# Loading the output gradient earlier, with rotating tables and four store buffers, in a spectral block's forward and backward kernel

## The chip, the cores and the metric

The kernel runs on one core of one Trainium2 chip. The metric is the time of one execution on the device in microseconds, lower is better. A core has TensorE (PE, with its weight loads shown as PEld), VectorE (DVE), ScalarE (ACT), GpSimd (POOL) and SyncE (SP), each working through its own list of instructions in order, and 16 DMA engines. Nearly all transfers of this kernel are issued from SP's queue.

## The reference

The reference computes one transformer-like block in bf16 and the gradients of all its weights and of its input. The sequence has 2048 rows of 512.

```
h = layernorm(x) * (1 + ca) + sa
x = x + ga * irfft2(rfft2(h) * (w_r + i w_i))        # spectral filter
h = layernorm(x) * (1 + cb) + sb
x = x + gb * (relu(h @ w1 + b1)**2 @ w2 + b2)        # MLP, 512 -> 1792 -> 512
sa, ca, ga, sb, cb, gb = split(silu(c) @ w_mod)      # modulation, six rows of 512
out, vjp = jax.vjp(block, x, w_r, w_i, w1, b1, w2, b2, c, w_mod)
return out, *vjp(grad_out)
```

The outputs that matter here: out_2 and out_3 are the gradients of w_r and w_i, out_4 that of w1, out_5 of b1, out_6 of w2, out_7 of b2, out_1 of x, out_9 of w_mod.

## The kernel before

Rows are laid on 128 partitions, 16 row tiles (NT) of 512 columns. The Fourier transforms are products with small tables. The kernel has these stages, in order of time.

1. To about 100 us: the first layer norm, the forward transforms and the product with the filter (`spec_f23`, `spec_g1`), filled with products of the transposed output gradient with w2 (L707).
2. To about 283 us: for each of four blocks of 512 rows, the inverse transform, the second layer norm, both products of the MLP and the backward of the MLP. The hidden layer and its gradient are stored to `h_dram` and `gh_dram`; the gradient's transposed blocks are loaded back (`ghn`, tiles named gab). The row gradients are kept in `gx1_dram`.
3. To about 337 us, the middle stage on the way back: `spec_f23` is called with `ew_b` and `after_b`. It has eight steps `gi`. In each, PE makes psB and psC (L323, L311), ACT copies them to AE and G (L329, L330, L313), and DVE multiplies G with the filter Z and with the saved spectrum Xt (`cmul`, L418 to L421). The products are stored as the gradients of w_r and w_i from tile gW (L1146). Around that PE works through units of the gradient of w1 (`grad_w1`, L1104), whose result ACT copies into gw1 tiles (L1108) of two units each; they are stored at L1110. Four of the six modulation gradients (`GMod.emit`) are made here, after steps 1, 3, 5 and 7. Each multiplies a broadcast row with w_mod's columns (tile wmc, DVE, L470) and writes an outer product (tile gwm, ACT and DVE, L467 and L469), with two loads and two stores.
4. To the end: `spec_g1` (L346), then eight steps of two row tiles (`row_pair`) with the last transforms (L375, L385), the layer norm's backward on DVE and ACT with the saved rows n1 and gxl (L1193, L1194), and a store of out_1. Around them stand the units of w2's gradient (`grad_w2`, L1173): each reads the whole output gradient `g_sb` (2 MB) and one transposed block of the hidden layer (`hn`, loaded with a transposing DMA at L1168), and DVE takes its PSUM result away (L1176). PSUM pool `mmps` has two buffers. The last two modulation gradients and the gradient of c end the kernel.

On-chip memory is nearly full, so pools are stacked from the left and from the right and re-used. A new pool on old space waits for everything in the pools that lay there. The pools that matter: `gap` (ghn), `gwa` (G, gw1, and the modulation tiles), `spb` (Z), `f23b` (Xb, four buffers), `ewb` (products and gW), `cdp` (Cd, AE and LF tables 0 to 3), `lf2` (LF tables 4 to 7, 6 KB a partition), `gwp` (g_sb with 16 KB a partition, hn, gw) and `fin` (n1, gxl). Pool `gwp` is opened after `lf2` is released, and lies in part where `ewb` was.

The order of instructions on each engine is drawn up at build by a planner: it goes by the order of the program, by priorities (`high_priority`, `Priority`), by when data and buffers come free in its own estimate of time, and by `issue_after`, which queues an instruction behind another on the same engine. On the chip each engine and SP's queue keep that order and wait in place.

Each LF table is read by the psC products of one step (L311). Tables 4 to 7 are loaded in `load(gi)`, which `after_b` calls four steps ahead; the first loads of Z and Xb come from the same function.

Of the kernel before, what the change touches and what calls it, by code (L numbers as in the profile page):

```python
# [12 lines left out]
BF16 = mybir.dt.bfloat16  # L13
# [5 lines left out]
D = 512  # L19
DF = 257  # L20
# [3 lines left out]
NT = 16  # L24
# [3 lines left out]
P = 128  # L28
# [24 lines left out]
class Priority:  # L53


    def __init__(self, tc, shift):
        self.tc, self.shift = tc, shift
# [335 lines left out]
def merge(main, *fills):  # L393

    fill = [f for fl in fills for f in fl]
    k = 0
    for i, m in enumerate(main):
        m()
        while k < len(fill) and k * len(main) < (i + 1) * len(fill):
            fill[k]()  # L400
            k += 1
# [42 lines left out]
class GMod:  # L444
# [2 lines left out]

    def __init__(self, tc, K, scf, gsc, wm_view, out9_view):
        self.__dict__.update(locals())
        self.bufs = 2  # L450

    def emit(self, jc, q, row, pool, ppool):

# [22 lines left out]
def kernel(  # L476
# [5 lines left out]
    nc = tc.nc  # L482
# [14 lines left out]
    g_view = grad_out.rearrange("b (p t) d -> p (b t) d", t=NT)  # L497
# [20 lines left out]
    K = build_basic(tc, constp)  # L518
    mmps = ctx.enter_context(tc.tile_pool(name="mmps", bufs=2, space=PSUM, side="right"))
# [242 lines left out]
    with tc.tile_pool(name="psR", bufs=1, space=PSUM) as psR, tc.tile_pool(name="psO", bufs=2, space=PSUM) as psO_pool, \  # L762
# [92 lines left out]
        def ghn_part(b, fc):  # L855

            if fc == 0:
                tl = gap.tile([P, NFC, SB], BF16, name="gab", bufs=4)
                ghn[b] = tl.rearrange("p a b -> p (a b)").rearrange("p (j f) -> p j f", f=F)
            nc.sync.dma_start(ghn[b][:, :, fc * P:(fc + 2) * P], gh_dram[fc * P:(fc + 2) * P, b * SB:(b + 1) * SB], transpose=True)  # L860
# [149 lines left out]
        for b in range(NB):  # L1010
            again0, again = f1_again(UT) if b == NB - 1 else ([], [])
            if b < NB - 1:
                m = stage_m(0) if b == 0 else []
                stage_h(b, m + stage_g(b + 1), 2 if b == 0 else 6)
            else:
                late.lag = 2
                stage_h(b, again0, 2)
            parts = [lambda fc=fc: ghn_part(b - 1, fc) for fc in range(0, NFC, 2)] if b > 0 else []
            if b < NB - 1:
                merge(stage_o(b), stage_m(b + 1) + [lambda: None] * 2)  # L1020
                if b == NB - 2:
                    UT = utcs.tile([P, 4, 16, NT, 8], BF16, name="utcs")
                merge(stage_gn(b, UT), parts + [lambda: None])
            else:
                w1p.release()
                cdp = tc.alloc_tile_pool(name="cdp", bufs=1, side="right")
                K["Cd"] = cdp.tile([P, D], BF16, name="Cdb")
                nc.sync.dma_start(K["Cd"], Cd_dram)
                AEs = make_ae(nc, cdp)
                K["LF"] = [cdp.tile([P, 2, 3, P], BF16, name=f"LFb{gi}") for gi in range(4)]  # L1030
                for gi in range(4):
                    nc.sync.dma_start(K["LF"][gi], LF_dram[:, 2 * gi:2 * gi + 2])
                merge(stage_gn(b, UT), [x for p in zip(again, parts + [lambda: None]) for x in p])
                w1tp.release()
                h2p = tc.alloc_tile_pool(name="h2p", bufs=1, side="right")
                h2_sb = h2p.tile([P, NT, D], BF16, name="h2_sb")
                nc.sync.dma_start(h2_sb, h2_dram)
                parts = [lambda fc=fc: ghn_part(b, fc) for fc in range(0, NFC, 2)]
                merge(stage_o(b), [x for p in zip([lambda: None] * 3 + [late_f1.flush] + [lambda: None] * 3, parts) for x in p])
# [7 lines left out]


    gm = GMod(tc, K, scf, gsc, wm_view, out9_view)
    lf2 = tc.alloc_tile_pool(name="lf2", bufs=1, side="right")  # L1050
    K["LF"] += [lf2.tile([P, 2, 3, P], BF16, name=f"LFb{gi}") for gi in range(4, 8)]
    W4 = 448
    NFB = F // W4
    gwa = tc.alloc_tile_pool(name="gwa", bufs=1)
# [43 lines left out]
    w1o = {}  # L1098

    def grad_w1(fb, dc):  # L1100
        fs = slice(fb * W4, (fb + 1) * W4)
        ps = mmps.tile([P, SB], FP32, name="mm")
        for t in range(NT):
            nc.tensor.matmul(ps[:, 0:W4], lhsT=h2_sb[:, t, dc * P:(dc + 1) * P], rhs=ghn[t // 4][:, t % 4, fs],  # L1104
                             start=(t == 0), stop=(t == NT - 1))
        if fb % 2 == 0:
            w1o[0] = gwa.tile([P, 2, W4], BF16, name="gw1", bufs=2)
        nc.scalar.copy(out=w1o[0][:, fb % 2, :], in_=ps[:, 0:W4])  # L1108
        if fb % 2 == 1:
            nc.sync.dma_start(out4_view[:, dc, (fb - 1) * W4:(fb + 1) * W4], w1o[0].rearrange("p a f -> p (a f)"))  # L1110
# [8 lines left out]
    def fill_w1(n):  # L1119
        for _ in range(n):  # L1120
            if units:
                units.pop(0)()

    gms = [lambda j=j, q=q, row=row: gm.emit(j, q, row, gwa, mmps)
           for j, q, row in ((5, 0, grow[0:1, :]), (2, 32, grow[32:33, :]), (3, 64, grow[64:65, :]), (4, 0, gcrow))]

    with tc.tile_pool(name="f23b", bufs=2) as fr, tc.tile_pool(name="ewb", bufs=2) as ew:
        Xt = {}

        def load(gi):  # L1130
            if gi >= 4:
                nc.sync.dma_start(K["LF"][gi], LF_dram[:, 2 * gi:2 * gi + 2])
            nc.sync.dma_start(Z[gi], wz_dram[:, gi])
            Xt[gi] = fr.tile([P, 2, 2, FP], BF16, name="Xb", bufs=4)
            nc.sync.dma_start(Xt[gi], xs_dram[:, gi])

        for gi in range(4):
            load(gi)

        def ew_b(gi, G):  # L1140
            cmul(nc, ew, Z[gi], G, Z[gi][:, :, 0, 0:DF], Z[gi][:, :, 1, 0:DF], True)
            gW = ew.tile([P, 2, 2, FP], BF16, name="gW", bufs=3)
            cmul(nc, ew, Xt[gi], G, gW[:, 0, :, 0:DF], gW[:, 1, :, 0:DF], True)
            for i, o in enumerate((out_2, out_3)):
                for p0_, n, rows_ in w_parts(o, gi):
                    nc.sync.dma_start(rows_, gW[p0_:p0_ + n, i, :, 0:DF])  # L1146

        def after_b(gi):
            if gi + 4 < 8:
                load(gi + 4)  # L1150
            if gi == 4:
                nc.sync.dma_start(K["LG"], LG_dram)
            fill_w1(2 if 0 < gi < 6 else 1)
            if gi % 2 == 1:
                gms.pop(0)()

        spec_f23(tc, K, UT, AEs, None, lambda gi: gwa.tile([P, 2, 2, FP], BF16, name="G", bufs=2), ew_b, after_b)
    lf2.release()
    gwp = tc.alloc_tile_pool(name="gwp", bufs=1, side="right")
    g_sb = gwp.tile([P, NT, D], BF16, name="g_sb")  # L1160

    hns, endp = [], {}

    def load_hn():
# [28 lines left out]
            nc.sync.dma_start(rows3[t][0], n1_dram[:, t:t + 2, :])  # L1193
            nc.sync.dma_start(rows3[t][1], gx1_dram[:, t:t + 2, :])  # L1194

    nc.sync.dma_start(g_sb, g_view)
    load_hn()
    load_rows3(0)
    load_rows3(2)
# [105 lines left out]
    fp.release()  # L1305
    fin.release()
    gwp.release()
    h2p.release()
    cdp.release()
    cfp.release()  # L1310
# [35 lines left out]
```

## Time and profile before

The median of 14 runs is 433.7 us (430.53 to 435.91).

| what | value |
|---|---|
| profiled execution, its own time | 435.66 us |
| its span, first to last instruction | 433.9 us |
| mean granted TensorE clock | 0.986 |
| busy: PE, DVE, ACT, POOL | 400.8, 353.7, 256.2, 41.1 us |
| DMA | 101.11 MB, mean 233 GB/s |
| L1173 (w2's gradient) on PE | 224 matmuls, 53.2 us |
| L1104 (w1's gradient) on PE | 256 matmuls, 51.4 us |

A row of the profile's groups names line, engine and operation, the tiles written and read, the count, busy time and mean duration, and the idle time just before these instructions with what ended it. In the rows of 40 slices one digit is the share of a slice of 10.8 us in tenths. Rows of the SP queue show when a DMA was issued and how long the issue took; the transfer lands later. An engine's idle time costs nothing where another engine sets the end.

### The profile page before, as it was taken

The page shows a single profiled execution, that of the slowest core. Times are in us where ns is not written, and L with a number is a line of the kernel's source. Part 1 is how long each engine was busy: PE and PEld are TensorE (multiplying, and loading weights), DVE is VectorE, ACT ScalarE, POOL GpSimd, SP SyncE. Part 2 cuts the span into 40 slices and gives each one's busy share as a digit, 9 for nine tenths or more (in the row PEclk, how much of TensorE's full clock was granted, in tenths as well). Part 3 has the DMA queues.
Part 4 walks back from the last instruction along what each step waited for, and adds up shares of the span by engine and source line. Part 5 has one row for each costly group of instructions (what it writes and reads, how often), then busy time and mean ns, then how long its engine had stood idle before and what let it go on. Part 6 is the DMA issues. An engine that isn't in the chain of part 4 may idle for free.

```text
span 433.9 us, 7120 instructions
## 1 busy us (share of the span) xinstructions
PE 400.8 (92%) x2375; PEld 196.9 (45%) x2375; DVE 353.7 (82%) x864; ACT 256.2 (59%) x487; POOL 41.1 (9%) x114
## 2 busy tenths in 40 slices
PE   2789999999899999999999999999999799994996
PEld 0344446654344434443444444455555464441332
DVE  6789768959995588969897998929568968978796
ACT  5578699679881286348536765465437466345231
POOL 8347930000000000000000000000000000000000
PEclk9999999999999999999999999999999999996899
DMA  9998899969595479669955997987995699999984
GB/s 241 238 287 256 240 229 306 308 234 193 177 358 191 121 146 326 173 156 233 295 171 158 218 339 268 235 246 208 266 304 148 184 278 250 209 251 266 259 216 138
DMA packets 147147, 101.11 MB, mean 233 GB/s; under 512 B 98945, under 2 KB 131590, under 8 KB 146726
## 3 DMA queue, kind: packets, MB, share of 16 engines
q1 hardware_dynamic: 145458, 98.01, 83.6%
q0 software_dynamic: 1088, 2.11, 2.1%
q10 hardware_dynamic: 564, 0.53, 0.4%
q8 instruction: 19, 0.31, 0.3%
q14 instruction: 18, 0.15, 0.1%
HBM read 35.44 MB, written 41.60 MB: 178 GB/s over the span
## 4 chain that ended last, share of the span: by engine, by line
PE 45%; DVE 20%; ACT 14%; DMA 9%; issue 4%; SPq 4%; POOL 1%; ACTq 0%; DVEq 0%
PE og L901 12%; PE mm L872 10%; PE mm L1173 6%; PE mm L707 5%; PE psG L346 3%; DVE gm_junk L470 3%; ACT gab L712 2%; PE mm L1104 2%; DMA n<-n_dram 2%; DMA h_dram<-h 1%; DMA out_dram<-gw 1%; ACT Xs L313 1%; ACT AE L329 1%; PE psY L385 1%; DMA Xb<-xs_dram 1%
## 5 line engine op out<-in xcount | busy, mean ns | idle before, releaser
L707 PE MATMUL mm<-gT,w2T 128*128 128x512 bf16 x224 | 57.8, 383 | 2.9 <-ACT gab L712 2.9
L1173 PE MATMUL mm<-g_sb,hn 128*128 128x512 bf16 x224 | 53.2, 393 | 3.0 <-DVE gw L1176 3.0
L872 PE MATMUL mm<-h2T,w 128*128 128x512 bf16 x224 | 53.4, 378 | 1.3 <-ACT r L874 1.2
L1104 PE MATMUL mm<-gab,h_sb 128*128 128x448 bf16 x256 | 51.4, 352 | 0.8 <-ACT gw L1108 0.8
L901 PE MATMUL og<-w1T,gab 128*128 128x512 bf16 x224 | 50.9, 379 | 0.8 <-DVE o L966 0.8
L901 PE MATMUL og<-w,h 128*128 128x512 bf16 x224 | 50.1, 379 | 0.0
L874 ACT ACTIVATE r<-mm,b1col 128x512 bf16<-128x512 f32 x56 | 37.0, 685 | 6.1 <-PE mm L872 3.3
L1173 PEld LDWEIGHTS <-hn 128*128 128x128 bf16 x224 | 21.7, 100 | 30.4 <-issue 8.4
L872 PEld LDWEIGHTS <-w 128*128 128x128 bf16 x224 | 21.1, 97 | 30.0 <-issue 8.3
L1104 PEld LDWEIGHTS <-h_sb 128*128 128x128 bf16 x256 | 24.6, 98 | 22.2 <-issue 1.6
L901 PEld LDWEIGHTS <-h 128*128 128x128 bf16 x224 | 21.8, 98 | 26.1 <-issue 0.9
L901 PEld LDWEIGHTS <-gab 128*128 128x128 bf16 x224 | 21.6, 98 | 25.9 <-issue 1.4
L707 PEld LDWEIGHTS <-w2T 128*128 128x128 bf16 x224 | 21.3, 99 | 22.4 <-issue 6.3
L914 ACT CAST G<-og 128x512 bf16<-128x512 f32 x16 | 9.2, 580 | 28.1 <-PE og L901 28.1
L876 DVE TENSOR_TENSOR h<-r 128x1024 bf16<-128x1024 bf16 x28 | 19.2, 684 | 4.8 <-ACT r L874 4.8
L712 ACT CAST gab<-mm 128x512 bf16<-128x512 f32 x36 | 21.3, 599 | 2.0 <-PE mm L707 1.8
L1108 ACT CAST gw<-mm 128x448 bf16<-128x448 f32 x16 | 8.7, 544 | 22.1 <-DMA out_dram<-gw 12.3
L1253 ACT ACTIVATE gs<-gn,inv 128x512 bf16<-128x512 bf16 x16 | 11.4, 716 | 17.3 <-DVE gn L1251 17.3
L418 DVE TENSOR_TENSOR p<-Z,G 128x1028 bf16<-128x1028 bf16 x8 | 5.6, 695 | 18.9 <-ACT G L313 10.6
L710 DVE CAST gab<-mm 128x512 bf16<-128x512 f32 x20 | 13.8, 688 | 8.0 <-PE mm L707 7.8
L377 ACT ACTIVATE Tsb<-psT 128x512 bf16<-128x512 f32 x32 | 18.5, 604 | 1.8 <-PE psT L375 1.5
L880 DVE TENSOR_TENSOR gab<-r,gab 128x1024 bf16<-128x1024 bf16 x28 | 19.1, 682 | 0.0
(289 smaller groups left out, 781.7 us busy)
## 6 DMA issues: line engine op xcount, KB each, us to landing
h_dram<-h SPq DMA_DIRECT2D x28, 256.0 KB, 3.3
gh_dram<-gab SPq DMA_DIRECT2D x28, 256.0 KB, 3.9
w<-in_B_w_dram SPq DMA_DIRECT2D x2, 1792.0 KB, 9.0
wmc<-in_w_mod_dram SPq DMA_DIRECT2D x12, 256.0 KB, 4.4
out_dram<-gwm SPq DMA_DIRECT2D x12, 256.0 KB, 3.1
wz_dram<-Z SPq DMA_DIRECT2D x8, 258.0 KB, 3.7
xs_dram<-Xs SPq DMA_DIRECT2D x8, 258.0 KB, 2.8
Z<-wz_dram SPq DMA_DIRECT2D x8, 258.0 KB, 4.4
```

Of the source, the lines that this page charges most:

```text
L346: nc.tensor.matmul(ps[:, ch, :], lhsT=Z[gi][:, hh, ri, ch:256:2], rhs=K["LG"][:, n, ri:ri + 2, :].rearrange("p y m -> p (y m)"), start=(ri ...
L377: nc.scalar.activation(Tsb, ps, AF.Copy, scale=EF_S)
L707: nc.tensor.matmul(ps, lhsT=w2T[:, dc, fc * P:(fc + 1) * P], rhs=gT[b][:, :, dc, :], start=(dc == 0), stop=(dc == 3))
L710: nc.vector.tensor_copy(out=gaT[b][:, fc, :], in_=ps)
L712: nc.scalar.copy(out=gaT[b][:, fc, :], in_=ps)
L872: nc.tensor.matmul(ps, lhsT=w1[:, dc, (fc + i) * P:(fc + i + 1) * P], rhs=h2T[b][:, :, dc, :], start=(dc == 0), stop=(dc == 3))
L874: nc.scalar.activation(r[:, i, :], ps, AF.Relu, bias=b1col[:, fc + i:fc + i + 1])
L876: nc.vector.tensor_tensor(h2, r, r, op=ALU.mult)
L880: K["gh"] = nc.vector.tensor_tensor(gh, r, gh, op=ALU.mult).ins
L901: nc.tensor.matmul(ps, lhsT=lhs(fc), rhs=rhs[:, fc, :], start=(fc == 0), stop=(fc == NFC - 1))
L1104: nc.tensor.matmul(ps[:, 0:W4], lhsT=h2_sb[:, t, dc * P:(dc + 1) * P], rhs=ghn[t // 4][:, t % 4, fs], start=(t == 0), stop=(t == NT - 1))
L1173: nc.tensor.matmul(ps, lhsT=hns[fc][:, t, :], rhs=g_sb[:, t, :], start=(t == 0), stop=(t == NT - 1))
```

## The change

- The modulation gradients take their tiles from `ew` (pool `ewb`) and no longer from `gwa`, with four buffers for wmc and gwm in place of two. The fourth is made after step 6, no longer after step 7.
- The LF tables 4 to 7 have no pool of their own. All LF tables are one rotating tile name with four buffers in `cdp`; table gi + 4 is allocated when its load is issued, and takes the place of table gi.
- A pool `gsp` stands where `lf2` stood; it holds `g_sb` from before the middle stage. Its load is issued in `after_b(5)`, queued on SP behind the last store of that step's gW. `gwp` no longer holds `g_sb`.
- The gw1 store tiles have four buffers in place of two.

```diff
@@ GMod.__init__
-        self.bufs = 2
+        self.bufs = 4
@@ the last block of stage 2
-                K["LF"] = [cdp.tile([P, 2, 3, P], BF16, name=f"LFb{gi}") for gi in range(4)]
+                K["LF"] = [cdp.tile([P, 2, 3, P], BF16, name="LFb", bufs=4) for gi in range(4)]
@@ ahead of the middle stage
-    lf2 = tc.alloc_tile_pool(name="lf2", bufs=1, side="right")
-    K["LF"] += [lf2.tile([P, 2, 3, P], BF16, name=f"LFb{gi}") for gi in range(4, 8)]
+    gsp = tc.alloc_tile_pool(name="gsp", bufs=1, side="right")
+    g_sb = gsp.tile([P, NT, D], BF16, name="g_sb")
@@ grad_w1
-            w1o[0] = gwa.tile([P, 2, W4], BF16, name="gw1", bufs=2)
+            w1o[0] = gwa.tile([P, 2, W4], BF16, name="gw1", bufs=4)
@@
-    gms = [lambda j=j, q=q, row=row: gm.emit(j, q, row, gwa, mmps)
+    gms = [lambda j=j, q=q, row=row: gm.emit(j, q, row, ew, mmps)
@@ load
             if gi >= 4:
+                K["LF"].append(cdp.tile([P, 2, 3, P], BF16, name="LFb", bufs=4))
                 nc.sync.dma_start(K["LF"][gi], LF_dram[:, 2 * gi:2 * gi + 2])
@@ ew_b
-                    nc.sync.dma_start(rows_, gW[p0_:p0_ + n, i, :, 0:DF])
+                    K["gW"] = nc.sync.dma_start(rows_, gW[p0_:p0_ + n, i, :, 0:DF]).ins
@@ after_b
             fill_w1(2 if 0 < gi < 6 else 1)
-            if gi % 2 == 1:
+            if gi == 5:
+                with tc.issue_after(K["gW"]):
+                    nc.sync.dma_start(g_sb, g_view)
+            if gi in (1, 3, 5, 6):
                 gms.pop(0)()
@@ after the middle stage
-    lf2.release()
     gwp = tc.alloc_tile_pool(name="gwp", bufs=1, side="right")
-    g_sb = gwp.tile([P, NT, D], BF16, name="g_sb")
@@
-    nc.sync.dma_start(g_sb, g_view)
     load_hn()
@@ the end
     gwp.release()
+    gsp.release()
```

## Prediction

> **What bounds the kernel now.** I read the page's totals first, then its row of slices, then stretches of the second half, the waits of the stages from 280 us on, and the SP queue in order of time.
>
> ```profile
> span 433.9 us, 7120 instructions
> PE 400.8 (92%) x2375; PEld 196.9 (45%) x2375; DVE 353.7 (82%) x864; ACT 256.2 (59%) x487; POOL 41.1 (9%) x114
> PE   2789999999899999999999999999999799994996
> PEclk9999999999999999999999999999999999996899
> DMA  9998899969595479669955997987995699999984
> ```
>
> TensorE is the bound nearly everywhere, so a change is worth only the idle and the slow clock that it takes from TensorE. In the second half two places show that: the slice at about 340 us, and the two at about 390 to 410 us, where the clock falls too. The DMA row is at 9 from about 350 us to 420 us.
>
> ```profile
> 328.00:332.00 4.00, 4.00 (x30) 2.41 (x29) 4.00 (x11) 3.38 (x7) 0.00 (x0) 1.00 0.24 75
> 340.00:344.00 4.00, 3.16 (x26) 1.87 (x26) 4.00 (x12) 1.21 (x3) 0.00 (x0) 1.00 0.33 75
> 348.00:352.00 4.00, 4.00 (x32) 2.95 (x31) 3.80 (x9) 3.09 (x6) 0.00 (x0) 1.00 0.83 332
> 396.00:400.00 4.00, 0.96 (x4) 0.32 (x3) 2.47 (x6) 3.45 (x8) 0.00 (x0) 0.50 1.06 202
> 400.00:404.00 4.00, 4.00 (x11) 1.07 (x10) 3.66 (x11) 0.57 (x1) 0.00 (x0) 0.50 1.07 335
> ```
>
> Each row is a stretch of 4 us: its length, then busy time of PE, PEld, DVE, ACT and POOL, the granted clock, the DMA share and GB/s. At 328 and 340 us the DMA engines are a quarter to a third busy; at 400 us PE is full of work at half clock.
>
> ```profile
> ACT gw L1108 <- DMA out_dram<-gw: 12.3, 2, 7.0
> DVE p L418 <- ACT G L313: 10.6, 2, 5.8
> DVE q L1254 <- DMA n<-n_dram: 5.5, 3, 3.0
> PE mm L1083 <- DVE gn L1262: 3.1, 1, 3.1
> PE mm L1173 <- DVE gw L1176: 3.0, 1, 3.0
> PE psG L346 <- DVE utcs L351: 2.1, 1, 2.1
> PE mm L1104 <- ACT gw L1108: 0.8, 1, 0.8
> ```
>
> Here are two chains of waits. ScalarE waits twice for a store of the first weight's gradient (12.3 us), VectorE waits behind it for G (10.6 us), and of this TensorE feels only 0.8 us at L1104 and 2.1 us at L346. Later VectorE waits for the loaded rows n, and TensorE stands twice for some 3 us because its PSUM results are not taken away.
>
> ```profile
> 346.75 0.35 SPq L1196 DMA_DIRECT2D g_sb<-in_grad_out_dram  x1
> 347.16 7.86 SPq L1168 DMA_TRANSPOSE hn<-h_dram  x1
> 355.07 0.57 SPq L1193 DMA_DIRECT2D n<-n_dram  x1
> 379.81 5.43 SPq L1168 DMA_TRANSPOSE hn<-h_dram  x2
> 385.34 0.53 SPq L1193 DMA_DIRECT2D n<-n_dram  x1
> 393.75 0.52 SPq L1193 DMA_DIRECT2D n<-n_dram  x1
> ```
>
> The 2 MB load of g_sb enters the queue at 346.75 us. The transpose behind it holds SP for 7.86 us, where the shortest of the 14 takes 2.13 us, so the queue stands 5.7 us for g_sb. The row loads n that VectorE waits for at 385.5 and 396.3 us sit behind such transposes.
>
> **The change, part by part.**
>
> **Four store buffers for gw1.** ACT's two waits (5.27 us at 302.5 and 7.02 at 317.8) go: a store starts every 7 us or so and lands in 3.9 us, and with four buffers one has more than 20 us. TensorE gets 0.8 us directly (bounds 0 and 0.8). VectorE loses its idle of 10.6 us, which pays in the next part.
>
> **The fourth modulation gradient one step earlier.** Its issues are one matmul on PE (0.38 us), three copies on ACT (1.9), six vector instructions on DVE (3.4), two loads and two stores on SP. It moves past eight matmuls of the last inverse step, ACT's two copies of G, the last cmul group on DVE and that group's four stores. Counting DVE from its first cmul at 290.98 us to the end of the last at 342.18 us gives 51.2; less 10.6 of waiting, plus 3.4 moved ahead, is 44.0, so it would be ready by 335.0. The last G is written by ACT at 334.9 us in either case, TensorE being full; the last cmul therefore runs from 334.9 to 338.7, and DVE's first eviction of psG, at 344.72 today, starts 6 us sooner. PE's 2.1 us at L346, and 0.3 beside it for ACT's evictions, can go; with 0.3 of issue idle the bounds are 0 and 2.7. I take 1.6, since eight evictions at 0.6 us still run on an in-order DVE that has other work. Without this cover (a DVE that stays late) the part is worth nothing.
>
> **Modulation tiles in the pool of the elementwise work, four buffers.** The two 256 KB loads issued at 282.15 us can no longer go out there: the new pool's space opens with the store that lands at 288.05. Their first reader on DVE stands at 298.5. Behind eight Z and Xb loads (issued 288.15 to 292.1) they should land at 296 to 303. If late, cmul of the next step is queued behind them on DVE; 10.6 us of freed slack covers that, so 0 (uncovered: up to 4.5). In the other direction the store at 283.14, which took 4.9 us against a median of 2.4 behind these loads, may land earlier; DVE starts sooner, PE is full there, 0.
>
> **LF tables rotate.** Four loads of 192 KB leave 281 to 285 us and go behind each step's stores, one per step. Each now waits for PE's matmuls of the step four before it, on SP; behind it stand that step's Z and Xb loads, which must wait for the same step's DVE work anyway. A table is used some 25 us after its slot opens and lands in 4.4 us: 0.
>
> **g_sb early.** One issue of 0.35 us on SP moves in front of two wmc loads, the gwm stores, a gw1 store and the last eight gW stores. It follows the gW stores of step 5, at 333.6 us today, at about 329 with ACT's wait gone. At the 332 GB/s of the stretch that it fills today it takes 6.3 us. The stretch 328 to 334 moves 83 GB/s. What it could hold up are the last gW stores, which open the space for hn, n and gxl. The Trainium skill (DMA: Bandwidth & Descriptors, Queues, rings and completion order) speaks against the move: one ring's descriptors are taken in order, and a completion lands after every earlier write of that engine. By the rule a gW store issued just after g_sb lands up to 6.3 us late; by the nearest row, the store at 283.14 behind some 1 MB, 2.5 us late. With g_sb gone by 336 and the last stores issued after 338.7, I take 0; if it slid to 338 us, the opening at 346.7 would move by 2.5 to 6.3.
>
> **What the last stage gains.** SP's queue runs 5.7 us ahead, and the engines have 2.1 MB less of 18.9 (346.7 to 421.5 us, share 1.04). The n loads of 385.34 and 393.75 come about 5 us sooner and land before DVE's 385.5 and 396.3, so DVE's 3.0 and 1.5 us go. On PE the idle after 390.7 is 6.1 us. Half clock lies on top: the 16 matmuls at 399.1 and 401.4 took 1.79 + 4.36 us, where full clock (0.216 each, from 3.45 us for 16) needs 3.46, so 2.7. The rule (TensorE: Matmul & The Clock Gate, Part 1) gives half speed until some 3.4 us of sustained work, a loss of 1.7. So PE could give 8.8 by the row and 7.8 by the rule; neither decides, because DVE has only 3.0 + 1.5 + 2.3 (its wait for the slow PE at 403.7) = 6.9 to give, and from 385.45 to 431 us it is busy 37.3 of 45.6 us. Bounds 0 and 6.9. I take the 4.5 of the n waits and 0.8 of the last: 5.3.
>
> **Sum:** 0.8 + 1.6 + 5.3 = 7.7 us. The profiled execution took 435.66 us (span 433.9, 1.8 around it), 2.0 above the runs' median of 433.7; the terms are differences, so 433.7 - 7.7 = 426.0. All upper bounds together, 0.8 + 2.7 + 6.9 = 10.4, would give 423.3; PE alone, 0.8 + 2.7 + 8.8 = 12.3, gives 421.4.
>
> **Rivals.**
> *Only the middle stage gains.* The last stage's DMA share stays near 1 without g_sb, and each n load still has one or two hn transposes in front (2.1 to 3 us each), so DVE waits as before. For: 16.8 MB remain. Against: 3.0 us of lateness is less than the 5.7 gained. 433.7 - 2.4 to 3.0: 431.
> *Nothing arrives.* PE has 52.7 busy of 53.5 us from 284 to 337.5; what DVE gains is waited away at the next TensorE result, and the last stage is paced by VectorE (65.4 of 75.4 us). Within 433.7 ± 1.3.
> *Slower: the replanned order lets TensorE meet hn too soon.* The order on each engine is drawn up at build from estimated times. With g_sb early, the planner may move a first group of L1173 (today at 360.0 us) ahead of the left-over L1104 groups and the psT and psY products. The first hn can't be issued before about 345, and hn lands up to 7.5 us after its issue: PE would stand at 350 until 353 or later, with everything behind it. If PE stands 6 us, the half clock adds 2.7, and with the late row pairs all behind, 433.7 - 0.8 + 6 + 2.7, some of it offset: 437 to 441. It decides from about 6 us of standing, which eats the sum less 1.6. Against: the left-over L1104 groups have 10 us of work ready.
>
> **How the numbers follow.** Both gains 0.54 (its own range 421.5 to 429.5), middle stage only 0.20, nothing 0.09, slower 0.17. A measurement here tells a difference of about 0.3%, 1.3 us. Faster is 0.54 + 0.20 = 0.74, same 0.09, slower 0.17. The range runs from 421.0, PE's floor, to 434.5, which takes in the first three cases and leaves out the slower one.
>
> **What would show it.** Right: no ACT wait on out_dram<-gw at L1108; L1196's load gone and a g_sb load at about 329 to 334 us; the first hn issue at 2 to 3 us; no n wait over 1 us on DVE; clock 1.0 through 390 to 410. Wrong: gW stores landing past 348, a DVE wait for wmc at the first gm_junk, or PE idle before its first L1173.

## The result, and the profile after

The changed kernel takes 437.65 us (median of 10 runs, 435.46 to 439.09) against 432.84 us for the kernel before beside it: a ratio of 1.0103, 95% interval 1.0078 to 1.0128. It is slower by about 4.5 us. The forecast was 426.0 us, faster: its sign was wrong.

The profiled execution took 437.68 us, with a span of 435.2 us and a mean clock of 0.984. Taking the moment at which the pool of the last stage opens (the first issue of g_sb or hn behind it) as the border, the trace of before has 346.75 us up to it and 87.15 us from it to the end; after has 354.20 and 81.0. The last stage gained 6.2 us and the part ahead of it lost 7.5. That makes 1.3 us between these two executions, less than the 4.5 of the ratio, because the profiled execution of before (435.66 us) lay 2.8 us above its median; a later execution of the changed kernel beside two of before (e16 with e14 and e15) has spans of 438.2 against 433.3 and 435.2.

In the listings of the changed kernel most line numbers of this part are larger by one than in the kernel before (hn is L1169, gW L1147, the products of w2's gradient L1174), and the load of g_sb is L1157.

The stretches of 4 us of the changed kernel, with the columns of the rows shown for before (length; busy PE, PEld, DVE, ACT, POOL; clock, DMA share, GB/s):

```profile
336.00:340.00 4.00, 1.25 (x7) 0.54 (x6) 3.61 (x9) 1.98 (x4) 0.00 (x0) 1.00 0.98 241
340.00:344.00 4.00, 3.14 (x15) 2.23 (x15) 4.00 (x12) 1.82 (x4) 0.00 (x0) 0.51 0.97 348
344.00:348.00 4.00, 3.92 (x48) 2.17 (x46) 4.00 (x10) 1.17 (x2) 0.00 (x0) 0.64 1.03 328
352.00:356.00 4.00, 3.27 (x18) 2.23 (x18) 3.81 (x9) 0.58 (x1) 0.00 (x0) 0.71 0.20 43
396.00:400.00 4.00, 2.48 (x12) 0.86 (x10) 3.93 (x12) 1.78 (x4) 0.00 (x0) 1.00 0.98 236
400.00:404.00 4.00, 3.52 (x19) 1.63 (x19) 3.56 (x8) 3.02 (x8) 0.00 (x0) 0.69 0.98 295
404.00:408.00 4.00, 4.00 (x20) 1.50 (x18) 3.44 (x11) 1.01 (x3) 0.00 (x0) 0.89 1.24 192
```

The quiet place that was to take the load is not quiet any more: at 336 us TensorE is busy for 1.25 of 4 us, then runs at a clock of 0.51 and 0.64. The half clock near 400 us, which stood in two rows of before, is down to rows of 0.69 and 0.89.

The waits of the changed kernel from 280 us on (engine, line, what it waited for: total, times, longest):

```profile
DVE gm_junk L470 <- DMA wmc<-in_w_mod_dram: 13.7, 4, 7.1
...
ACT gmbc L459 <- DVE gm_junk L470: 8.4, 2, 4.5
...
PE psG L346 <- ACT G L313: 3.6, 1, 3.6
...
PE psG L346 <- DVE utcs L351: 2.0, 1, 2.0
```

Two rows of before are gone: ScalarE's 12.3 us for stores of gw, and VectorE's waits for the rows n (in the second execution, e16, 3.0 us of these are back, the longest 1.5). In their place VectorE stands 13.7 us for w_mod columns, for which the trace of before has no such row (two more executions of before have 0.7 and 0.6 us). The rows of VectorE's own timeline show where:

```profile
307.79 0.75 DVE L470 SCALAR_TENSOR_TENSOR gm_junk<-wmc,onef,gmbc 128x512 bf16<-128x512 bf16 x1 [3.01 <-DMA wmc<-in_w_mod_dram]
323.26 0.75 DVE L470 SCALAR_TENSOR_TENSOR gm_junk<-wmc,onef,gmbc 128x512 bf16<-128x512 bf16 x1 [7.11 <-DMA wmc<-in_w_mod_dram]
336.36 0.75 DVE L470 SCALAR_TENSOR_TENSOR gm_junk<-wmc,onef,gmbc 128x512 bf16<-128x512 bf16 x1 [0.77 <-DMA wmc<-in_w_mod_dram]
351.31 0.75 DVE L470 SCALAR_TENSOR_TENSOR gm_junk<-wmc,onef,gmbc 128x512 bf16<-128x512 bf16 x1 [2.78 <-DMA wmc<-in_w_mod_dram]
```

Each of the four modulation gradients waits. The queue of SP says why (issue time, length of the issue):

```profile
303.85 0.39 SPq L463 DMA_DIRECT2D wmc<-in_w_mod_dram  x1
...
319.11 1.10 SPq L463 DMA_DIRECT2D wmc<-in_w_mod_dram  x2
...
336.50 0.58 SPq L1157 DMA_DIRECT2D g_sb<-in_grad_out_dram  x1
337.20 2.00 SPq L472 DMA_DIRECT2D out_dram<-gwm  x2
...
346.81 0.38 SPq L463 DMA_DIRECT2D wmc<-in_w_mod_dram  x1
...
349.36 2.51 SPq L1147 DMA_DIRECT2D out_dram<-gW  x4
354.20 1.98 SPq L1169 DMA_TRANSPOSE hn<-h_dram  x1
```

The first w_mod load goes out at 303.85 us, where before it went at 282.15. Its reader stands at 304.8. It is not the space that holds it: VectorE writes the first product in the same pool at 288.60. The load stands in SP's order behind the Z and Xb loads, behind ten gW stores of the first two steps and behind the loads and stores between them; why the planner put it there is not shown. The g_sb load comes at 336.50, not at 329, because the gW stores ahead of it come from a VectorE that is late; and the two gwm stores are directly behind it. The last four gW stores go from 349.36 on (before: the last eight from 338.18 to 344.45), and the first hn at 354.20. Its issue takes 1.98 us where it took 7.86.

The chain that ended last, in the same stretch:

```profile
332.20 4.06 DMA wmc<-in_w_mod_dram
...
337.20 9.60 DMA out_dram<-gwm
346.81 4.47 DMA wmc<-in_w_mod_dram
351.31 0.76 DVE gm_junk L470 x2
352.07 0.61 DVE utcs L351
352.69 0.04 issue
352.73 0.60 PE psG L346 x4
```

A 256 KB store that took 3.1 us in the median of before takes 9.60 us behind the 2 MB load. The load itself lands after 9.6 us, at 346.1, and the store 0.7 us behind it. The next w_mod load leaves SP only when the store has landed, although neither touches the other's data. VectorE waits 2.78 us for that load, and TensorE behind VectorE 2.0 us at psG, until 352.73. This second stand is the big load's.

The first and longer stand comes before it, as the timelines of ScalarE and TensorE show:

```profile
338.02 0.58 ACT L459 CAST gmbc<-mm 128x512 bf16<-128x512 f32 x1 [4.54 <-DVE gm_junk L470]
338.50 0.60 ACT L313 CAST G<-psC 128x514 bf16<-128x514 f32 x1
...
340.86 3.57 PE L346 MATMUL psG<-LGb,Z 128*128 128x256 bf16 x16 [3.61 <-ACT G L313]
```

The fourth gradient's gmbc has one buffer and must wait for the third gradient's last read of it, which is late: that read is on VectorE, behind the waits for w_mod at 323.26 and 336.36. G of the last step is behind gmbc on ScalarE, and TensorE stands 3.61 us from 337.25 on, after which 16 matmuls take 3.57 us where they took 1.92. The g_sb load was issued less than 1 us before TensorE stood, and the store behind it landed 6 us after the stand was over; so this stand belongs to the late w_mod loads and to the place of the fourth gradient, not to the big load. From 336 to 356 us PE is busy 14.3 us (17.5 before), and the rows of 0.51, 0.64 and 0.71 plus the one of 0.86 at 356 us hold 4.5 us of lost clock: together 7.6 of the 7.7 us by which the first psT product is later (360.68 against 352.99).

### The profile page after: what moved, and what is told of

It reads as the page before. It is cut to its first block, busy times and chain, and to the rows that moved or that the text cites. A ratio compares the mean times of both kernels' runs of the same rounds, so it can differ in the third digit from the quotient of the medians.

```text
span 435.2 us, 7116 instructions
## 1 busy us (share of the span) xinstructions
PE 403.1 (93%) x2375; PEld 198.4 (46%) x2375; DVE 354.3 (81%) x864; ACT 256.7 (59%) x487; POOL 41.2 (9%) x114
## 4 chain that ended last, share of the span: by engine, by line
PE 41%; DVE 25%; ACT 15%; DMA 10%; issue 5%; SPq 1%; POOL 1%; ACTq 0%; DVEq 0%
PE og L901 11%; PE mm L872 10%; PE mm L707 5%; DMA wmc<-in_w_mod_dram 4%; PE mm L1104 3%; DMA xs_dram<-Xs 2%; DMA out_dram<-gwm 2%; DVE gm_junk L470 2%; ACT gab L712 2%; PE mm L1174 2%; DVE jk L1258 2%; PE psG L346 2%; ACT AE L329 1%; ACT Xs L313 1%; ACT Tsb L377 1%
## 5 line engine op out<-in xcount | busy, mean ns | idle before, releaser
L1104 PE MATMUL mm<-gab,h_sb 128*128 128x448 bf16 x256 | 52.3, 354 | 0.0
L1174 PE MATMUL mm<-g_sb,hn 128*128 128x512 bf16 x224 | 51.5, 385 | 0.0
L1104 PEld LDWEIGHTS <-h_sb 128*128 128x128 bf16 x256 | 24.7, 98 | 21.1 <-issue 0.6
L1174 PEld LDWEIGHTS <-hn 128*128 128x128 bf16 x224 | 21.5, 100 | 26.2 <-issue 3.3
L470 DVE SCALAR_TENSOR_TENSOR gm_junk<-wmc,onef,gmbc 128x512 bf16<-128x512 bf16 x24 | 17.9, 747 | 14.5 <-DMA wmc<-in_w_mod_dram 13.7
L353 ACT CAST utcs<-psG 128x512 bf16<-128x512 f32 x16 | 9.4, 585 | 16.8 <-PE psG L346 16.8
L346 PEld LDWEIGHTS <-Z 128*128 128x128 bf16 x128 | 14.0, 112 | 11.2 <-DVE Z L420 3.9
```

Of the source, the lines that this page charges most:

```text
L346: nc.tensor.matmul(ps[:, ch, :], lhsT=Z[gi][:, hh, ri, ch:256:2], rhs=K["LG"][:, n, ri:ri + 2, :].rearrange("p y m -> p (y m)"), start=(ri ...
L470: nc.vector.scalar_tensor_tensor(out=junk, in0=wmc[:, i, :], scalar=K["onef"], in1=gmbc, op0=ALU.mult, op1=ALU.mult, accum_out=self.gsc[:, ...
L1174: nc.tensor.matmul(ps, lhsT=hns[fc][:, t, :], rhs=g_sb[:, t, :], start=(t == 0), stop=(t == NT - 1))
```

## The experiments

Theories. **W**: the move of the gradients' tiles into pool `ewb` makes the w_mod loads late. **G**: the 2 MB load delays the small stores behind it. **S**: the fourth gradient, right behind the third, waits at its single gmbc. The rivals of each stand in the expectations. All ratios are to the kernel before beside the same runs.

**e1: w_mod tiles back in the earlier pool.**

```diff
-            wmc = pool.tile([P, 2, D], BF16, name="wmc", bufs=self.bufs)
+            wmc = (wpool or pool).tile([P, 2, D], BF16, name="wmc", bufs=2 if wpool else self.bufs)
@@ gms
-    gms = [lambda j=j, q=q, row=row: gm.emit(j, q, row, ew, mmps)
+    gms = [lambda j=j, q=q, row=row: gm.emit(j, q, row, ew, mmps, gwa)
```

> The changed kernel with one thing put back: the wmc tiles come from gwa again (two buffers), whose space opens some 4 us earlier than ewb's; everything else as changed. Theory W (late loads of w_mod set the loss: they are issued at 303.9 us instead of 282.2 and VectorE stands 13.7 us for them): its waits on wmc fall below 3 us, g_sb is issued at 328 to 332 us, TensorE's standing at 337 goes, time 426 to 430. Theory G (the early 2 MB load holds the small stores and loads behind it): wmc waits of the first two gradients go, but a store behind g_sb still lands after 8 us or more, 434 to 437. Theory S (the fourth gradient right behind the third holds ScalarE on its one gmbc buffer, so the last G is late): ScalarE still waits some 4 us at L459 and TensorE some 3.5 us at L346, 434 to 437.

Measured 1.0072 (1.0049 to 1.0096), 436.42 us. The first loads go out at 282.15 us again and the first gradient's wait is gone, but the others remain (11.4 us in all), since the second gradient's loads are issued at 313.28 only. TensorE's stand for tile G falls from 3.61 to 0.9 us. W in this form is worth about 0.3% of the 1.0%, and as the two intervals overlap, this difference is not clear of the noise.

**e2: the g_sb load back at its old place in the program.**

```diff
@@ after_b
-            if gi == 5:
-                with tc.issue_after(K["gW"]):
-                    nc.sync.dma_start(g_sb, g_view)
@@ after the middle stage
+    nc.sync.dma_start(g_sb, g_view)
```

> The changed kernel with g_sb's load back at its old place behind the middle stage; its pool stays. W: the waits on the first two gradients' wmc stay at 10 us in sum, TensorE still stands at 337, 436 to 440. G: the 9.6 us landing of the gwm store goes, 431 to 434. S: TensorE still stands at 337, 435 to 439.

Measured 1.0134 (1.0090 to 1.0177). This run did not do what its name says. As g_sb keeps its pool of its own, which is free early, the planner put the load at 281.15 us, ahead of the first Z load, which moved to 291.6. It is slower than e1, e3 and e4: VectorE waits 14.9 us for w_mod and ScalarE 9.5 us at one gmbc, TensorE 8.2 us at psG. But it is no clean test against G, because the load now stands ahead of everything else in the stage: VectorE waits 11.5 us for the first Z and starts at 294.33, where it starts at 288.60 in the changed kernel. That the loss does not need an early load is shown by e5 below.

**e3: the fourth gradient back after step 7.**

```diff
-            if gi in (1, 3, 5, 6):
+            if gi in (1, 3, 5, 7):
```

> The changed kernel with the fourth modulation gradient back behind step 7. W: waits on wmc stay above 10 us, 435 to 439. G: g_sb is still issued at about 336, 435 to 438. S: ScalarE's wait at L459 ahead of the last G goes, so TensorE's 3.6 us at L346 and the half clock after it go, 431 to 434.

Measured 1.0106 (1.0079 to 1.0133): no different from the change. TensorE's 3.6 us at G go and return as 4.0 us at psF and 2.1 at psG, all behind a VectorE that waits 15.1 us for w_mod. S is the place where the lateness surfaced, and taking it away alone wins nothing.

**e4: before with the early load and the rotating tables alone** (tiles in `gwa` with two buffers, two gw1 buffers, gradients after 1, 3, 5, 7).

> The kernel before with only the early load of g_sb and the rotating LF tables that make its space: gradients in gwa with two buffers after steps 1, 3, 5 and 7, two gw1 buffers. W: VectorE never waits for wmc; ScalarE's 12.3 us on gw1 stores stay; the last stage gains what was forecast, 5 us, 427 to 430. G: g_sb issued at about 334 delays the last gW stores and the fourth gradient's loads, 433 to 437. S says as W.

Measured 1.0002 (0.9971 to 1.0032). Its chain, and two of its waits:

```profile
333.75 10.83 DMA out_dram<-gwm
...
345.85 1.86 PE psG L346 x8
```

```profile
PE psG L346 <- ACT utcs L353: 6.4, 1, 6.4
ACT gwm L467 <- DMA out_dram<-gwm: 6.0, 1, 6.0
```

The load goes out at 332.22 and the third gradient's stores right behind it. ScalarE waits 6.0 us for one of their two buffers and TensorE stands 6.4 us. So G exists, and in this kernel nothing is won.

**e5: before with the tiles in `ewb` alone** (two buffers of each).

```diff
-    gms = [lambda j=j, q=q, row=row: gm.emit(j, q, row, gwa, mmps)
+    gms = [lambda j=j, q=q, row=row: gm.emit(j, q, row, ew, mmps)
```

> The kernel before with one edit: the modulation tiles come from the pool of the elementwise work, still two buffers of each; store buffers, tables, gradient steps and the g_sb load stay. Theory W (the pool move is what loses the time: the first w_mod loads can go out only when that pool opens, about 304 instead of 282 us, and stand behind other transfers): VectorE waits over 8 us at the first gm_junk of its gradients, TensorE idles 3 to 5 us more in the middle stage, total 436 to 439. Theory G (the early 2 MB load holds up the small stores of the modulation gradient behind it, and nothing else matters much): VectorE's waits for w_mod are there too, but VectorE has room for them, and the total stays within 432 to 434.5.

Measured 1.0122 (1.0057 to 1.0188, four runs): by itself the pool move loses about as much as the whole change. The first w_mod load leaves at 307.22 us. The waits, and then the chain:

```profile
ACT gw L1108 <- DMA out_dram<-gw: 12.5, 2, 6.5
...
DVE gm_junk L470 <- DMA wmc<-in_w_mod_dram: 6.3, 3, 4.1
...
PE mm L1104 <- ACT gw L1108: 4.4, 2, 4.2
```

```profile
313.56 5.92 DMA out_dram<-gw
...
320.17 9.16 PE mm L1104 x32
```

Here, with two gw1 buffers, the loss comes out at another place than in the changed kernel: ScalarE waits for a store of gw that lands after 5.92 us, TensorE stands 4.2 us at L1104, and the next 32 matmuls take 9.16 us where 32 took 6.05 us just before. ScalarE's waits for gw stores are in sum as long as before (12.5 against 12.3 us), and before has a wait of 7.0 us that costs TensorE 0.8 only; what differs is how much work TensorE has at that moment. With four gw1 buffers this wait is gone, as the changed kernel shows. So the move of the tiles is shown to cost time by itself. That it does so through late w_mod loads is shown in the changed kernel, where they stand in the chain; in e5 no w_mod load stands in it between 283 us and the opening of the last stage, and how the move leads to the stand at L1104 stays open.

**e6: e4 with the gradients after steps 1, 2, 3, 4; e7: e4 with g_sb in four parts; e8: both.**

```diff
@@ e6, e8
-            if gi in (1, 3, 5, 7):
+            if gi in (1, 2, 3, 4):
@@ e7, e8
-            if gi == 5:
+            if 2 <= gi < 6:
+                k = 4 * (gi - 2)
                 with tc.issue_after(K["gW"]):
-                    nc.sync.dma_start(g_sb, g_view)
+                    nc.sync.dma_start(g_sb[:, k:k + 4, :], g_view[:, k:k + 4, :])
```

> e4_gsb_alone (before with g_sb loaded early and tables that rotate), and the four modulation gradients are made after steps 1, 2, 3, 4 instead of 1, 3, 5, 7, so that none of their small loads and stores stands behind the g_sb load on SP. Theory G: e4's 6.4 us of TensorE idle at psG and the half clock behind it go, the last stage's gain of about 6 us stays, total 426 to 429.5; the gwm stores land in under 5 us each. Rival (the last stage's gain is only the middle stage's loss seen at another place, since all transfers share one capacity): the idle time goes to another wait, total 432 to 434.5. Second rival (gradients this close wait for one another at their single-buffered tiles): ScalarE waits at gmbc and TensorE stands 2 to 4 us between 300 and 330, total 430 to 433.

> e4_gsb_alone, with g_sb loaded in four parts of 512 KB, one each behind the gW stores of steps 2, 3, 4 and 5, and gradients after steps 1, 3, 5, 7 as before. Theory G (it is the mass of bytes directly ahead of the gwm stores that counts): a gwm store waits for at most one part, some 1.6 to 2.5 us more than in the kernel before, so lands in 4 to 6 us, TensorE idle at psG falls from 6.4 to under 3 us, total 427 to 431. Rival (any load ahead costs the same, or the parts delay the Z and Xb loads of the next steps instead): TensorE waits for Z or psF over 3 us, total 433 or more.

> Both: g_sb in four parts behind steps 2 to 5, and the gradients after steps 1, 2, 3, 4. Theory G: as e6 or up to 1 us slower, since gradients after steps 2, 3 and 4 now stand behind one part each, 426 to 430. Rival (crowding of the queue between 300 and 330 us): VectorE waits over 6 us for w_mod loads there, total 431 to 435.

Measured 1.0031 (1.0006 to 1.0055), 1.0148 (1.0098 to 1.0199) and 1.0078 (1.0056 to 1.0099). All three miss what G promised. Their totals go with the rivals or above them, but the waits that the rivals named came only in part. In e6 the gradients crowd: ScalarE waits 11.7 us at gmbc and g_sb slides to 342.45 us. In e7 the parts stand ahead of gw stores: ScalarE waits 15.9 us for them (longest 10.6), and TensorE stands 7.0 us at L1104, not for Z or psF. In e8 TensorE stands 3.9 us for gmbc, and the pool opens at 357.28. Four smaller parts of the load were worse here than the one whole load (e7 against e4, e8 against e6).

**e9 and e18: e4 with the load behind the third gradient's stores. e10: e4 with the third gradient one step earlier. e11: the changed kernel with e1's edit and e9's. e12: e4 with the load on ScalarE's queue.**

```diff
@@ e9, e18; e11 in the same way with its (1, 3, 5, 6)
+            if gi in (1, 3, 5, 7):
+                gms.pop(0)()
             if gi == 5:
-                with tc.issue_after(K["gW"]):
+                with tc.issue_after(K["gwm"]):
                     nc.sync.dma_start(g_sb, g_view)
-            if gi in (1, 3, 5, 7):
-                gms.pop(0)()
@@ e10
-            if gi in (1, 3, 5, 7):
+            if gi in (1, 3, 4, 7):
@@ e12
-                with tc.issue_after(K["gW"]):
-                    nc.sync.dma_start(g_sb, g_view)
+                with tc.issue_after(K["gwc"]):
+                    nc.scalar.dma_start(g_sb, g_view)
```

`K["gwm"]` is the gwm store issued last in the program, `K["gwc"]` the copy of ScalarE into gw1 that was made last.

> e4_gsb_alone (before with g_sb loaded early and tables that rotate) with the g_sb load put behind the third gradient's two gwm stores on SP instead of ahead of them; behind it stand the gW stores of the last two steps and the fourth gradient's transfers. Theory G (a small store directly behind the 2 MB load lands 8 us late and TensorE stands for it): e4's 6.4 us of TensorE idle at psG and the half clock behind it go, the gwm stores of the third gradient land in 3 to 5 us, the last stage keeps 5 to 6 us; total 426 to 430, ratio 0.985 to 0.993. Rival (the delay only passes to the gW stores behind the load, which open the space for hn): the first hn goes out 4 to 6 us later than in the kernel before's order would allow, TensorE stands less but the end gains nothing; ratio 0.997 to 1.005.

> e9_gsb_behind_gwm again, beside e17 on one chip. If its trace of 430.9 us was a quick draw: ratio 1.000 to 1.004 as before, and from the first hn issue to the end 83 to 86 us instead of 82.3. If the early load does win where nothing stands behind it in the middle stage: ratio 0.992 to 0.997. Against e17: if four store buffers are worth the predicted 0.8 us, e17 is 0.1 to 0.3 per cent below this one with the same place of the fourth gradient.

> e4_gsb_alone with the third gradient one step earlier (gradients after steps 1, 3, 4, 7), so that its loads and stores are ahead of the g_sb load on SP, and only gW stores and the last gradient's stores behind. Theory G: as e9, 426 to 430, ratio 0.985 to 0.993. Rival (two gradients within a step of each other wait for one another at their single gmbc and for w_mod loads, as seen where all four were crowded): VectorE waits over 5 us for w_mod between 315 and 330 us, TensorE stands 3 to 5 us there; ratio 1.000 to 1.008.

> The changed kernel with two things mended: the w_mod tiles taken from the earlier pool with two buffers (as in e1_wmc_early), and the g_sb load behind the third gradient's gwm stores. Theory W with G (late w_mod loads and stores held behind the big load are the whole loss): e1's ratio of 1.007 falls by what G costs there, some 3 to 6 us of 436, to 0.993 to 1.000. Rival (the other tiles of the gradients in the pool of the elementwise work keep the last stage from opening, and four store buffers bring nothing): stays at 1.004 to 1.010.

> e4_gsb_alone with the g_sb load issued from ScalarE's queue instead of SP's, behind the gradient copy that ScalarE makes at about 329 us, so at the same time but on another ring. Theory G by ring order (a completion on a ring lands after every earlier write of the same ring): the gwm stores behind it on SP land in 3 to 5 us though both share the 16 engines, TensorE's 6.4 us go, ratio 0.985 to 0.993. Rival (shared bandwidth: what delays the stores is that the engines are full of the 2 MB, whatever the ring): gwm stores take 6 to 11 us as in e4 and the ratio stays at 0.997 to 1.004.

e9 measured 1.0023 (0.9996 to 1.0050), e18, the same kernel, 1.0015 (0.9991 to 1.0039). TensorE's 6.4 us at psG are down to 2.2 + 0.3 us in both, as before the change, so G's place is mended; still no time is won. e18's chain shows what stands there instead:

```profile
338.90 6.12 DMA out_dram<-gW
345.03 4.97 DMA out_dram<-gW
...
350.08 1.98 SPq L1169
```

Now the gW stores behind the load are late (6.12 us; the median of before is 3.3), and they open the pool: it opens at 348.6 and 350.1 us. In both, TensorE also stands 1.9 us for hn near 399 us, as in no trace of before. The two traces of this one kernel have spans of 430.9 and 433.0 us, so a gain of 2 us read from one trace means nothing here.

e10 measured 1.0041 (1.0018 to 1.0065), in the rival's range, but with other waits than the rival named: VectorE waits 4.2 us for w_mod in the whole stage, and TensorE stands 3.5 us at psG at 349 us and not between 315 and 330.

e11 measured 0.9985 (0.9954 to 1.0017), 432.93 us. Two edits take the changed kernel from 1.0103 to the time of before: the w_mod tiles in the earlier pool (to 1.0072) and the load behind the gwm stores (to 0.9985, 3.8 us). The second edit without the first was not run, so how the loss divides between them is known in this order only. VectorE still waits for w_mod, but less:

```profile
DVE gm_junk L470 <- DMA wmc<-in_w_mod_dram: 8.8, 2, 5.4
...
ACT gmbc L459 <- DVE gm_junk L470: 2.1, 1, 2.1
```

8.8 us is under the 10.6 us of VectorE's waiting for G in before, and 13.7 us is over it. This fits the two results but is not a rule: e5 waits 6.3 us for w_mod and loses 1.2%.

e12 measured 1.0078 (1.0054 to 1.0101), against the expectation by ring order and above the rival's range too. The chain of e12:

```profile
334.02 8.48 DMA out_dram<-gwm
...
343.76 1.44 PE psG L346 x6
```

The store is on SP's ring and the load, issued at 329.13, on ScalarE's, and still the store takes 8.48 us and TensorE stands 4.4 us. So the delay of the store does not need the order of one ring; it goes with the 2 MB on the same engines. Why e12 is slower than e4 (1.0002) was not followed.

**e13: before with the rotating tables alone; e14, e15: before again; e16: after again.** Here the question was whether the gain read in the last stage was one execution's luck.

> The kernel before with the rotating LF tables alone; g_sb stays late, so this is e4_gsb_alone without its early load. If the rotation costs nothing, as the prediction took it: ratio 0.997 to 1.003, and the early load of e4 is worth nothing by itself. If the rotation costs (its loads stand ahead of each step's Z and of the second gradient's w_mod loads): ratio 1.005 to 1.012, and the early load in e4 was worth 2 to 5 us that the rotation ate.

> The kernel before, profiled in another execution. Theory D (the two stands of TensorE near 391 and 399 us, the half clock at 400 us and the n waits of 3.0 and 1.5 us belong to the one execution that was profiled, whose clock of 0.986 is below the 0.992 that most executions of before have): from the issue of g_sb to the end 82 to 85 us instead of 87.2, clock of the span 0.99 or more, no row of half clock near 400. Theory P (they are the kernel's): 86 to 88 us, the half-clock row there again.

> The kernel before in a third execution, for the same question: theory D 82 to 85 us from the issue of g_sb to the end, and the length of that part differs between executions by 2 us or more; theory P 86 to 88 us in each.

> The changed kernel in another execution. Theory W with G: the first w_mod loads go out at about 304 us again, VectorE waits 12 to 16 us for w_mod, TensorE stands 4 to 7 us before psG and psF or at L1104 between 336 and 358 us, and from the first hn issue to the end 79 to 82 us, as in the execution profiled first. Rival (the first execution was a slow draw of this kernel too): w_mod waits under 8 us and TensorE stands under 3 us there.

e13 measured 1.0007 (0.9976 to 1.0038): no cost of the rotation is seen. e14 and e15 show the same last stage as the execution that the forecast read; TensorE stands 6.3 and 5.6 us in it and the half clock is back (stretches of e14):

```profile
392.00:396.00 4.00, 2.42 (x11) 0.63 (x11) 4.00 (x12) 1.53 (x4) 0.00 (x0) 0.59 1.16 238
396.00:400.00 4.00, 0.65 (x7) 0.49 (x5) 1.35 (x4) 3.46 (x8) 0.00 (x0) 0.50 0.75 164
```

So theory D falls: these stands are the kernel's. From the opening to the end they have 86.4 and 85.4 us, D's 82 to 85 not reached. e16 repeats the changed kernel's pattern: w_mod waits of 16.1 us, TensorE 5.3 + 3.4 us at psG, opening at 356.0, then 82.2 us.

**e17: e11 with the fourth gradient after step 7.**

> e11_after_mended with the fourth modulation gradient back after step 7, so that it stands behind the last gW stores on VectorE and SP. It differs from e9_gsb_behind_gwm in the four store buffers for gw1 and in the place of the gradients' other tiles. If the fourth gradient a step earlier is worth what the prediction took (1.6 us), the ratio rises from e11's 0.9985 to about 1.002; if it only delays the last gW stores, which open the space for hn, the ratio falls to 0.992 to 0.996 and the first hn goes out 2 to 4 us sooner than e11's 350.8 us.

Measured 1.0031 (1.0009 to 1.0053), against 0.9985 for e11. The queue of e17:

```profile
351.32 0.44 SPq L472 DMA_DIRECT2D out_dram<-gwm  x1
356.19 2.50 SPq L1169 DMA_TRANSPOSE hn<-h_dram  x1
```

With its tiles in `ewb`, a gradient made after the last step keeps that space in use: the last gwm store goes at 351.32, and hn at 356.19 where e11 has 350.79. The earlier step is worth some 2 us in this setting (the two intervals just overlap), though e3 found it worth nothing where VectorE is late anyway. e17 also answers what was asked of it beside e18: four store buffers were to put it 0.1 to 0.3 per cent below e18, and it lies 0.16 above (1.0031 against 1.0015), though its last stage also opens 6.1 us later.

The opening of the last stage and the rest, by trace, and the ratios by runs:

| kernel | opening, us | opening to end | ratio |
|---|---|---|---|
| before (three executions) | 346.8, 346.9, 349.8 | 87.2, 86.4, 85.4 | 1 |
| e13, tables alone | 348.0 | 84.5 | 1.0007 |
| e5, tiles alone | 355.0 | 85.7 | 1.0122 |
| e4, early load and tables | 349.5 | 83.6 | 1.0002 |
| e9, e18, load behind gwm stores | 348.6, 350.1 | 82.3, 82.9 | 1.0023, 1.0015 |
| e11, after mended | 350.8 | 80.4 | 0.9985 |
| e10, third gradient earlier | 355.1 | 78.2 | 1.0041 |
| e17, e11 with the fourth after step 7 | 356.2 | 79.0 | 1.0031 |
| after (two executions) | 354.2, 356.0 | 81.0, 82.2 | 1.0103 |

The early load is worth, at openings that are near to each other (e4, e9, e18 against before and e13), 82.9 against 85.9 us in the mean: 2.9 us, while the opening itself comes 1.5 us later (349.4 against 347.9). The 1.4 us left in the traces are not seen in the runs, whose ratios are 1.0002 to 1.0023; where that remainder goes stays open, and it is smaller than the 2.1 us between two traces of one kernel. No version beats the kernel before by more than the interval allows.

## Why the prediction was wrong, step by step

**Four store buffers for gw1, −0.8: the waits went as forecast, the gain is not shown.** ScalarE's waits for gw stores are gone in the changed kernel, and so is the wait at L1104. What they are worth alone was not tried, and e17 beside e18 shows no gain.

**Fourth gradient a step earlier, −1.6: wrong in the changed kernel; the size came once, by luck.** It was worth nothing there (e3). The some 2 us of e11 against e17 come by another path than the step's: TensorE waits 1.5 us at psG in e11 and 1.4 in e17, and what differs is the opening, 350.8 against 356.2. The step assumed that VectorE would be ready by 335.0; the condition it named itself ("a DVE that stays late") held. Its own single gmbc was overlooked: ScalarE waits 4.54 us there, ahead of the last G.

**Modulation tiles in the elementwise pool, 0: the step that failed.** The working let the w_mod loads go at some 292 us, behind eight Z and Xb loads, and land by 303. The time at which the space opens was read well enough; the place in the queue was not. The loads stand behind the first gW stores and the next step's loads as well, and go at 303.85. The step covered the wait with 10.6 us of freed VectorE time; it measured 13.7 us, and it comes at all four gradients where the step counted the first. In place of 0, the edit alone cost 5.3 us (e5: 1.22% of 436; 2.5 to 8.2 by its interval), near the stated price without cover, up to 4.5 us, though in e5 by another path.

**g_sb early, 0: failed too.** The step took 6.3 us for the load; where a trace gives its landing it took 8.9 to 11.8 us (e18, after, e9, e16, e1). It listed the gwm stores among what the load passes, then priced the last gW stores only. The stores directly behind are the gwm stores, and they land after 9.60 us (10.83 in e4), which is 6.5 to 7.7 us more than their median. The rule weighed there (the Trainium skill, DMA: Bandwidth & Descriptors, Queues, rings and completion order) gave 6.3 us, the row 2.5, and 0 was taken: the rule came close, and the store that lands 0.7 us after the load agrees with it. The prediction named one ring; the section says that a completion lands after every earlier write of that DMA engine "across its queues", and e12's 8.48 us on another ring agree with that, not with the expectation by ring order. The same section also says that an engine takes turns between rings packet by packet; an estimate by that, the store at half rate, would be twice 3.1, 6.2 us, still under the measured time. Putting the load behind those stores gained 3.8 us from e1 to e11 and nothing from e4 to e9; there the gW stores inherited the wait. The step's own condition ("if it slid to 338 us") also came close: it slid to 336.5, and to 338.0 in e16.

**LF rotation, 0: right** within the 0.4% that e13 can tell.

**Last stage, −5.3: sign right, size too large.** In the two traces of after it is 4.7 us shorter than in the three of before (81.6 against 86.3), but part of this comes with a later opening: e10, which opens at 355.1, has 78.2. At a like opening 2.9 us are measured. All of it, and more, is spent ahead of the opening.

**The rivals.** The slower one's time, 437 to 441, holds the result, its mechanism does not: TensorE nowhere stands for hn in the changed kernel near 350 us. It stood at 337 us, for ScalarE and behind it for VectorE; the half clock that this rival added to the stand did come. In e9 and e18 a stand for hn does come, but near 399 us and of 1.9 us. "Nothing arrives" describes e4, e9 and e11. "Only the middle stage gains" is the reverse of what came. Of the signs named, two of the wrong ones came true (last gW stores issued up to 351.9, a wait for wmc at the first gm_junk), and so did three of the five right ones: no ACT wait for gw stores, the first hn issue at 1.98 us, no n wait over 1 us (1.5 in e16). The load came at 336.5 instead of 329 to 334, and the clock dips to 0.69 at 400 us. The signs that came right were signs of the gain; the wrong ones were those of its price.

## What to carry to other kernels

A stretch with idle DMA engines is not a place where a big load is free: look up which small transfers stand directly behind it in the queue, and who waits for each; here they were 256 KB stores, and moving the load behind two of them was worth 3.8 us in one kernel (e1 to e11) and nothing in another (e4 to e9), where the next stores waited instead. When tiles move to another pool, their loads can move much further in the queue than the space opens later (here 21.7 us, with the space open by 288.60): read the issue time of each load and compare it with its reader, for every use and not only the first. A slack freed on one engine covers one lateness, not each of those that the same change brings, so sum the claims on it before calling several edits free.

## What the hardware showed that was not expected

A 256 KB store issued within 2 us of a 2 MB load on the same ring landed after 9.60 and 10.83 us (median 3.1), in the first case 0.7 us after the load, and after 8.48 us when the load had been issued 4.9 us ahead of it on another engine's ring; changing the ring gained nothing (1.0078 against 1.0002). After TensorE stood 3.61 us its clock was 0.51 and 0.64 for two stretches of 4 us, with work to do in both, and after a stand of only 2.0 us 0.71 and 0.86 (in e1, 0.60 after a stand of 1.99 us); in this execution standing cost nearly as much again (4.5 us of clock on 5.6 us of standing). The prediction's 1.7 us a stand would make 3.4. A load on SP left only when a store issued 9.6 us before it had landed, without sharing data with it (346.81 us in the changed kernel, and the same at 347.76 in e16): as far as the profile can tell, a late store can hold the queue itself.
